# Chunks of 384 tokens in a fused attention and FFN kernel

## The chip, the cores and the metric

The kernel runs on one core of one Trainium2 chip. The metric is the device time of one execution in microseconds (us). A core has these engines, each with an in-order list of instructions of its own: TensorE (PE in the profile, with its weight loads as PEld), VectorE (DVE), ScalarE (ACT), GpSimd (POOL) and SyncE (SP), which here issues DMAs. Semaphores order them against each other.

## What is computed

```python
phi(x) = exp(h - max(h)) / sqrt(m)        # h = x*scale @ omega.T - |x*scale|^2/2, m = 128 features
kv  = phi(k)^T v                          # per batch and head, 128 x 64
z   = sum over s of phi(k)
att = phi(q) kv / (phi(q) . z + 1e-6)     # q, k, v: 8 batches, 8 heads, 576 tokens, 64 dims
x   = att as (4608 tokens) x (512 = heads x dims)
h   = x @ w_in                            # 512 -> 2048
out = (h - tanh(h)) @ w_out               # 2048 -> 512
```

All is fp32; a product of two fp32 matrices is made of three matmuls of rounded parts (hi x hi, hi x lo, lo x hi), so that most tiles have a hi and a lo (`xh` and `xl`, `gh` and `gl`, `qh` and `ql`).

## The kernel before

The FFN goes through the 4608 tokens in chunks of 256 (chunks 0 and 1 together, then 2 to 17). For a chunk, DFF = 2048 is cut into 16 slices `f` of 128 rows, taken two at a time (`s` from 0 to 7). For each `s`, `ffn_p` makes h of two slices in one PSUM bank (256 tokens each, 24 matmuls of 256 columns), `ffn_g` makes g = h - tanh(h) and its parts gh and gl on ACT and DVE (tanh, subtract, round, subtract), and `ffn_out` adds them to the two output tiles po0 and po1 (128 tokens x 512, 12 matmuls of 512 columns). In the loop, `ffn_out` of a step stands behind `ffn_h` of the next one: h(s+1), then out(s). Behind the last step of a chunk `ffn_store` copies the output tiles and stores them.

The attention of the next chunks runs beside it, in pieces that are generators. A `q_unit(ch, c)` makes the x of chunk `ch` for a pair of heads `c` (four pairs): it loads q, splits it in hi and lo (`split_rows`), projects it (`features`: pj on PE, a copy on ACT, a reduction on DVE, Exp on ACT), multiplies with z for the denominators `dn` on DVE, normalizes, transposes (pt on PE, then qh and ql), multiplies with kv (pn on PE, then copies and adds to `xs`), and `x_split` writes xh and xl. A `k_unit(b, c)` makes kv and z of a batch and a pair in a like way (ka, km and kb are its projections, khl and vhl its parts, pk its sums). Each `beat()`, two in a step, moves every open generator by one `yield`; the table `start` says at which beat a unit begins. x has two buffers, by the parity of the chunk.

The order on each engine is not the order of the code: up to the 14th slice of chunk 0 it is written out by hand (`ORDER`), and behind that a scheduler orders the instructions ahead of time, by its own estimate of when each is ready; on the chip every engine takes its list strictly in that order. PSUM has eight banks: h0 and h1 for h, po0 and po1 for the outputs, and for attention pj0 and pj1 (projections), pt (shared by pt and pn) and pk.

Of the kernel before, what the change touches and what calls it, by code (L numbers as in the profile page):

```python
# [81 lines left out]
def favor_attention_ffn(ctx: ExitStack, tc: tile.TileContext, qT, kT, va, vt, omT, w, out):  # L82
# [84 lines left out]
    def features(lhs, name):  # L167

        n = len(lhs)
        ph = att("phi", [P, 4, M], F32, f"phi_{name}")  # L170
        nb = sb.tile([P, 4], F32, tag="nb", name=f"nb_{name}", bufs=12)

        for g in range(0, n, 2):
            m = min(2, n - g)
            pj = ps.tile([P, 2, 2 * M], F32, tag=bank("pj"), name=f"pj_{name}_{g}")
            for i in range(m):
                nc.tensor.matmul(pj[:, i], lhs[g + i], om2, start=True, stop=True)  # L177
            nc.scalar.copy(ph[:, g : g + m], pj[:, :m, M:])  # L178
            for i in range(m):
                j = g + i  # L180
                nc.vector.tensor_tensor_reduce(  # L181
                    ph[:, j], pj[:, i, :M], ph[:, j], scale=-SCALE, scalar=3.0e38,
                    op0=ALU.add, op1=ALU.min, accum_out=nb[:, j : j + 1])
        for j in range(n):
            nc.scalar.activation(ph[:, j], ph[:, j], AF.Exp, bias=nb[:, j : j + 1], scale=-1.0)  # L185
        return ph
# [107 lines left out]

    def q_unit(ch, c):

        n = f"{ch}_{c}"
# [8 lines left out]
        ix = lambda h, t: 2 * h + t
        dn = sb.tile([P, 4], F32, tag="dn", name=f"dn_{n}", bufs=8)
        for h in range(2):
            for t in range(2):
                i = ix(h, t)  # L310
                for b, s, e in pieces:
                    s, e = max(s, t * P), min(e, (t + 1) * P)
                    if s < e:
# [1 line left out]
                        nc.vector.tensor_tensor_reduce(  # L315
                            bank("junk")[r], ph[r, i], kvs[b, c][1][r, h], scale=1.0, scalar=EPS,
                            op0=ALU.mult, op1=ALU.add, accum_out=dn[r, i : i + 1])
        nc.vector.reciprocal(dn, dn)
        nc.vector.tensor_mul(ph, ph, dn.rearrange("p (i o) -> p i o", o=1).to_broadcast([P, 4, M]))
# [4 lines left out]
        for i in range(4):
            nc.tensor.transpose(pt[:, i * P : (i + 1) * P], ph[:, ix(i // 2, i % 2)], ident)  # L325
# [4 lines left out]
        nc.vector.tensor_sub(ql, pt2, qh.bitcast(F32))  # L330
        yield
        pn = ps.tile([P, 2, TC], F32, tag=bank("pt"), name=f"pn_{n}")
        for h in range(2):
            for b, s, e in pieces:
                w = kvs[b, c][0][:, h * P : (h + 1) * P]
                nc.tensor.matmul(pn[:, h, s:e], w, qh[:, h, s:e], start=True, stop=False)  # L336
                nc.tensor.matmul(pn[:, h, s:e], w, ql[:, h, s:e], start=False, stop=True)  # L337
# [8 lines left out]
        xdone[ch] = xdone.get(ch, 0) + 1

    def x_split(ch, c, x, engine):
        nc.scalar.copy(xh[:, ch % 2, c], x)
        engine.tensor_sub(xl[:, ch % 2, c], x, xh[:, ch % 2, c].bitcast(F32))  # L350
# [10 lines left out]
    xh, xl = [sb.tile([P, 2, NC, TC], F32R, name=f"x{k}") for k in "hl"]  # L361

    def ffn_p(ch, s, tag):

        p = ps.tile([P, 2, TC], F32, tag=tag, name=f"h_{ch}_{s}")
        for j in range(1 if ch == 0 else 2):
            f = s if ch == 0 else 2 * s + j
            o = p if ch == 0 else p[:, j]
            r = slice(0, 2) if ch == 0 else ch % 2
            prods = [(wt[f][:, i, c * P : (c + 1) * P], x[:, r, c]) for c in range(NC)  # L370
                     for i, x in ((0, xh), (0, xl), (1, xh))]
            for i, (w_, x) in enumerate(prods):
                nc.tensor.matmul(o, w_, x, start=i == 0, stop=i == len(prods) - 1)  # L373
        return p

    def ffn_g(ch, s, p):

# [6 lines left out]
        nc.scalar.copy(gh, g)  # L384
# [10 lines left out]
    def ffn_out(ch, s, gh, gl):  # L395
        po = pos[ch]
        for t in range(len(po)):
            for j in ((t // 2,) if ch == 0 else range(2)):
                f = s if ch == 0 else 2 * s + j
                h = gh[:, j, t % 2 * P : (t % 2 + 1) * P]  # L400
                l = gl[:, j, t % 2 * P : (t % 2 + 1) * P]
# [1 line left out]
                nc.tensor.matmul(po[t], h, wt[f][:, 0, DM:], start=first, stop=False)  # L403
# [5 lines left out]
    def ffn_store(ch):  # L409
        for t, p in enumerate(pos[ch]):  # L410
            if ch == NCH - 1 and t == 1:
                o = sb.tile([P, DM], F32, tag="g", name=f"o_{ch}_{t}")
                nc.vector.tensor_copy(o, p)
            else:
                o = sb.tile([P, DM], F32, tag="o", name=f"o_{ch}_{t}")
                nc.scalar.copy(o, p)
            r = ch * TC + t * P
            nc.sync.dma_start(out[r : r + P, :], o)
# [126 lines left out]
    def native_q(ch, c):  # L545
# [47 lines left out]
        def x_hi():  # L593
# [3 lines left out]
            if c < 2:  # L597
                x2[c] = sb.tile([P, TC], F32, tag="xs", name=f"x2_{c}", bufs=2)
            elif 2 not in x2:
                o = sb.tile([P, DM], F32, tag="o", name="x2")  # L600
                x2[2], x2[3] = o[:, 0:TC], o[:, TC:]
            nc.scalar.copy(x2[c], u["pn"])
# [227 lines left out]
```

## Time and profile before

| what | value |
|---|---|
| median of 3 runs | 1062.15 us (1059.04 to 1064.06) |
| the profiled execution | 1060.27 us |
| its span, first to last instruction | 1058.5 us |
| mean granted TensorE clock | 0.995 |
| first h of chunk 2 / chunk 3 / chunk 4 | 174 / 229 / 290 us |
| last matmul | 1054 us |

The profile is of one execution. Its rows give, for a group of instructions, line, engine, operation, tiles out and in, shape and count, then the busy time, the mean of one in ns, and the idle time of the engine ahead of them with what ended it. In a timeline a row begins with start and duration in us. Matmuls are pipelined: a row's duration is longer than the distance from its start to the next one, and the distance is what the engine needs for it.

### The profile page before, as it was taken

The page shows a single profiled execution, that of the slowest core. Times are in us where ns is not written, and L with a number is a line of the kernel's source. Part 1 is how long each engine was busy: PE and PEld are TensorE (multiplying, and loading weights), DVE is VectorE, ACT ScalarE, POOL GpSimd, SP SyncE. Part 2 cuts the span into 40 slices and gives each one's busy share as a digit, 9 for nine tenths or more (in the row PEclk, how much of TensorE's full clock was granted, in tenths as well). Part 3 has the DMA queues.
Part 4 walks back from the last instruction along what each step waited for, and adds up shares of the span by engine and source line. Part 5 has one row for each costly group of instructions (what it writes and reads, how often), then busy time and mean ns, then how long its engine had stood idle before and what let it go on. Part 6 is the DMA issues. An engine that isn't in the chain of part 4 may idle for free.

```text
span 1058.5 us, 20071 instructions
## 1 busy us (share of the span) xinstructions
PE 1038.0 (98%) x6908; PEld 938.4 (89%) x6908; DVE 804.0 (76%) x2761; ACT 679.8 (64%) x1730; POOL 276.4 (26%) x445
## 2 busy tenths in 40 slices
PE   9999998999999999999999999999999999999998
PEld 7777677988999999999999998999999999999997
DVE  6888765766688886789899878998888887666522
ACT  7996665665576755576667766676777675555422
POOL 1127650001133410234333334343333331000000
PEclk9999999998999999999999999999999999999999
DMA  8998562100011110011111111111101010000000
GB/s 232 278 247 253 128 157 61 57 31 10 17 53 30 46 31 33 11 48 33 54 33 53 33 43 39 33 54 33 46 30 45 30 37 11 30 16 21 1 21 20
DMA packets 43462, 64.67 MB, mean 61 GB/s; under 512 B 18656, under 2 KB 28000, under 8 KB 41312
## 3 DMA queue, kind: packets, MB, share of 16 engines
q1 hardware_dynamic: 38672, 38.19, 12.1%
q10 hardware_dynamic: 2384, 16.81, 4.5%
q0 software_dynamic: 2304, 8.39, 4.3%
q8 instruction: 55, 0.90, 0.3%
q14 instruction: 47, 0.39, 0.1%
HBM read 45.55 MB, written 9.44 MB: 52 GB/s over the span
## 4 chain that ended last, share of the span: by engine, by line
PE 82%; DVE 7%; ACT 4%; issue 3%; DMA 2%; POOL 1%; DVEq 0%; ACTq 0%; POOLq 0%; SPq 0%
PE h L373 34%; PE po L403 11%; PE po L404 11%; PE po L405 11%; PE pj_q L177 3%; PE pt L325 2%; PE pk L236 2%; DMA w<-a 2%; PE pn L337 2%; PE pn L336 2%; DVE a L650 1%; ACT k_phi L491 1%; DVE a L658 1%; PE pj_ka L177 1%; PE pj_kb L177 1%
## 5 line engine op out<-in xcount | busy, mean ns | idle before, releaser
L373 PE MATMUL h<-xh,w 128*128 128x256 f32 (+1 forms) x2176 | 451.9, 292 | 3.7 <-DVE g L381 2.5
L373 PEld LDWEIGHTS h<-xh,w 128*128 128x128 f32 x2176 | 357.4, 192 | 14.2 <-DVE g L381 2.7
L373 PE MATMUL h<-xl,w 128*128 128x256 f32 (+1 forms) x1088 | 317.7, 292 | 0.6 <-DVE xl L350 0.6
L403 PE MATMUL po<-w,gh 128*128 128x512 f32 x544 | 213.9, 393 | 1.6 <-ACT gh L384 1.6
L373 PEld LDWEIGHTS h<-xl,w 128*128 128x128 f32 x1088 | 208.8, 192 | 7.1 <-DVE xl L350 0.9
L404 PE MATMUL po<-w,gh 128*128 128x512 f32 x544 | 213.6, 393 | 0.0
L405 PE MATMUL po<-w,gl 128*128 128x512 f32 x544 | 211.8, 391 | 1.4 <-DVE gl L387 1.4
L384 ACT CAST gh<-g 128x512 fp32r<-128x512 f32 x144 | 89.4, 621 | 100.0 <-DVE g L381 98.6
L381 DVE TENSOR_TENSOR g<-h,g 128x512 f32<-128x512 f32 x144 | 98.9, 687 | 67.5 <-ACT g L379 66.3
L379 ACT ACTIVATE g<-h 128x512 f32<-128x512 f32 x144 | 85.5, 594 | 99.6 <-PE h L373 93.3
L387 DVE TENSOR_TENSOR gl<-g,gh 128x512 fp32r<-128x512 f32 x144 | 109.0, 757 | 42.5 <-ACT gh L384 40.7
L405 PEld LDWEIGHTS po<-w,gl 128*128 128x128 f32 x544 | 102.3, 188 | 24.5 <-DVE gl L387 3.7
L403 PEld LDWEIGHTS po<-w,gh 128*128 128x128 f32 x544 | 102.5, 188 | 18.4 <-ACT gh L384 2.0
L404 PEld LDWEIGHTS po<-w,gh 128*128 128x128 f32 x544 | 102.5, 188 | 15.5
L185 ACT ACTIVATE phi_q<-phi_q,nb_q 128x128 f32<-128x128 f32 x240 | 78.8, 392 | 3.7 <-DVE nb_q L181 3.5
L330 DVE TENSOR_TENSOR ql<-pt,qh 128x512 fp32r<-128x512 f32 x60 | 41.2, 686 | 38.1 <-ACT qh L329 37.9
L315 DVE CUSTOM_DVE_ANT_0 junk<-phi_q,zb 128x128 f32<-128x128 f32 (+1 forms) x200 | 59.9, 300 | 11.3 <-ACT phi_q L185 0.3
L241 POOL TENSOR_TENSOR zt<-phi_ka 128x256 f32<-128x256 f32 x20 | 16.9, 846 | 184.6 <-ACT phi_ka L185 184.6
L638 POOL TENSOR_SCALAR a<-a 128x1024 f32<-128x1024 f32 x14 | 53.1, 3799 | 32.1 <-ACT a L627 32.0
L181 DVE CUSTOM_DVE_ANT_0 phi_q<-pj_q,phi_q 128x128 f32<-128x128 f32 x240 | 55.8, 283 | 5.5 <-ACT phi_q L178 5.4
L329 ACT CAST qh<-pt 128x512 fp32r<-128x512 f32 x60 | 35.0, 583 | 38.7 <-PE pt L325 38.5
L228 POOL CAST vhl<-v 128x128 fp32r<-128x128 f32 (+1 forms) x120 | 37.3, 313 | 77.6 <-PE pk L236 73.0
(158 smaller groups left out, 1846.7 us busy)
## 6 DMA issues: line engine op xcount, KB each, us to landing
raw<-w ACTq DMA_DIRECT2D x16, 1024.0 KB, 6.3
out<-o SPq DMA_DIRECT2D x36, 256.0 KB, 2.0
w<-a POOLq DMA_DIRECT2D x16, 512.0 KB, 5.7
qf<-qT SPq DMA_DIRECT2D x60, 128.0 KB, 2.1
kf<-kT SPq DMA_DIRECT2D x20, 288.0 KB, 2.8
v<-vt SPq DMA_DIRECT2D x20, 288.0 KB, 2.8
v<-va SPq DMA_DIRECT2D x12, 320.0 KB, 4.6
k_f<-kT SPq DMA_DIRECT2D x12, 288.0 KB, 3.9
```

Of the source, the lines that this page charges most:

```text
L181: nc.vector.tensor_tensor_reduce(ph[:, j], pj[:, i, :M], ph[:, j], scale=-SCALE, scalar=3.0e38, op0=ALU.add, op1=ALU.min, accum_out=nb[:, ...
L185: nc.scalar.activation(ph[:, j], ph[:, j], AF.Exp, bias=nb[:, j : j + 1], scale=-1.0)
L315: nc.vector.tensor_tensor_reduce(bank("junk")[r], ph[r, i], kvs[b, c][1][r, h], scale=1.0, scalar=EPS, op0=ALU.mult, op1=ALU.add, accum_ou ...
L373: nc.tensor.matmul(o, w_, x, start=i == 0, stop=i == len(prods) - 1)
L379: nc.scalar.activation(g, p, AF.Tanh)
L381: nc.vector.tensor_sub(g, p, g)
L384: nc.scalar.copy(gh, g)
L387: nc.vector.tensor_sub(gl, g, gh.bitcast(F32))
L403: nc.tensor.matmul(po[t], h, wt[f][:, 0, DM:], start=first, stop=False)
L404: nc.tensor.matmul(po[t], h, wt[f][:, 1, DM:], start=False, stop=False)
L405: nc.tensor.matmul(po[t], l, wt[f][:, 0, DM:], start=False, stop=last)
L638: engine.tensor_scalar(u["af"], u["af"], -TOP, TOP, op0=ALU.max, op1=ALU.min)
```

## The change

Chunk 2 keeps its 256 tokens; behind it ten chunks (3 to 12) have 384. For them

- h of one slice fills a bank: 12 matmuls of 384 columns, 16 steps a chunk, where there were 24 of 256 for two slices and 8 steps;
- a chunk has three output tiles, po0, po1 and pj1, with 9 out matmuls a step. Attention keeps three banks: pj0, pt and pk;
- a `q_unit` has 384 tokens: three rounds of projection through pj0, each in a beat of its own, and pt, pn, copy and add for each head of the pair in turn through the bank pt;
- one tile each takes the place of several small ones (`zf`, `zr`: ident, junk, g, gh, gl, o, xs and others are slices of them), and most attention tiles have one buffer: qf one and not two, xs one and not two, phi two for q and one each for k's;
- the starting beats are new: chunk `ch` begins at beat 32 ch - 48, and its four q units at 32 ch - 87 + 8 c.

```diff
-NS = NF // 2
 TC = 256
-NCH = NT // TC
+TW = 384
+START = [0, TC, 2 * TC, *range(3 * TC, NT, TW)]
+NCH = len(START)
+WB = TW // P
...
 def features(lhs, name):
     n = len(lhs)
-    ph = att("phi", [P, 4, M], F32, f"phi_{name}")
+    kind, w = ("phq", 2 * WB) if name[0] == "q" else ("phm", 1) if n == 1 else ("phk", 4)
+    ph = att(kind, [P, w, M], F32, f"phi_{name}")
     for g in range(0, n, 2):
+        if g:
+            yield
...
 def q_unit(ch, c):
-    x = att("qx", [P, 2, TC], F32R, f"qx_{n}")
+    if ch > 3:
+        yield
+    x = att("qx", [P, 2, TW], F32R, f"qx_{n}")
...
-    pt = ps.tile([P, 2 * TC], F32, tag=bank("pt"), name=f"pt_{n}")
-    for i in range(4):
-        nc.tensor.transpose(pt[:, i * P : (i + 1) * P], ph[:, ix(i // 2, i % 2)], ident)
+    xs = zf[:, 8 : 8 + WB]
     for h in range(2):
+        pt = ps.tile([P, TW], F32, tag=bank("pt"), name=f"pt_{n}_{h}")
+        for t in range(WB):
+            nc.tensor.transpose(pt[:, t * P : (t + 1) * P], ph[:, 2 * t + h], ident)
+        nc.scalar.copy(qh, pt)
+        nc.vector.tensor_sub(ql, pt, qh.bitcast(F32))
+        yield
+        pn = ps.tile([P, TW], F32, tag=bank("pt"), name=f"pn_{n}_{h}")
         for b, s, e in pieces:
-            nc.tensor.matmul(pn[:, h, s:e], w, qh[:, h, s:e], start=True, stop=False)
-            nc.tensor.matmul(pn[:, h, s:e], w, ql[:, h, s:e], start=False, stop=True)
+            nc.tensor.matmul(pn[:, s:e], w, qh[:, s:e], start=True, stop=False)
+            nc.tensor.matmul(pn[:, s:e], w, ql[:, s:e], start=False, stop=True)
+        nc.scalar.copy(xs[r], blocks(pn)[o])
+        nc.vector.tensor_add(xs[r], blocks(pn)[r], xs[r])
+        yield
...
-    phi=(ak, 3), qh=(ak, 1), ql=(ak, 1), tmp=(ak, 1), kf=(ak, 1), kx=(ak, 1), qf=(ak, 2),
+    phq=(ak, 2), phk=(ak, 1), phm=(ak, 1), qh=(ak, 1), ql=(ak, 1), kf=(ak, 1), kx=(ak, 1), qf=(ak, 1),
...
-        k = [28,30,33,35][c] if ch == 3 else [42,45,48,52][c] if ch == 4 else 16 * (ch - 1) - 6 + 4 * c
+        k = [28, 31, 34, 37][c] if ch == 3 else 32 * ch - 87 + 8 * c
...
-        k = 28 + 5 * c if b == 2 else 16 * (need[b] - 1) - 25 + 8 * c
+        start.setdefault(48 * b - 89 + 12 * c, []).append(("k", b, c))
...
 for ch in range(2, NCH):
-    out_tiles(ch)
-    for s in range(NS):
+    if ch == 3:
+        mode.update(pj=["pj0"])
+    out_tiles(ch, ("po0", "po1") if ch == 2 else ("po0", "po1", "pj1"))
+    for s in range(8 if ch == 2 else NF):
```

How it moves instructions shows best where a chunk begins. PE before, from the last out matmuls of chunk 6 into chunk 7 (`po1_6` is an output tile of chunk 6, `h_7_1` the second step of chunk 7; all of `h_7_0` stands ahead of these rows):

```order
L404 MATMUL po1_6_4795<-w15_1760,gh_6_7_5423 128x512
L336 MATMUL pn_8_0_5532<-qh_8_0_5473,kvw_3_0_3281 128x256
L337 MATMUL pn_8_0_5532<-ql_8_0_5474,kvw_3_0_3281 128x256
L336 MATMUL pn_8_0_5532<-qh_8_0_5473,kvw_3_0_3281 128x256
L337 MATMUL pn_8_0_5532<-ql_8_0_5474,kvw_3_0_3281 128x256
L405 MATMUL po1_6_4795<-w15_1760,gl_6_7_5425 128x512
L373 MATMUL h_7_1_5613<-xh_100,w2_497 128x256
L373 MATMUL h_7_1_5613<-xl_101,w2_497 128x256
```

PE after, at the entry into its chunk 7: the last out matmul of chunk 6 (`pj1_6`) stands some rows ahead of these, and so do the products of `h_7_0` and `h_7_1` with pairs 0 to 2; `pt_7_3` and `pn_7_3` make the x of pair 3, `pj_kb5_1` and `pk_5_1` belong to k of batch 5, and the two rows of L403 are the first products of h with pair 3:

```order
L335 MATMUL pt_7_3_0_6399<-zf_68,phi_q7_3_6270 128x128 x3
L184 MATMUL pj_kb5_1_0_6471<-om_96,kx_5_1_6280 128x256 x2
L243 MATMUL pk_5_1_6303<-khl_5_1_2_6373,vhl_5_1_2_6374 128x256 x2
L243 MATMUL pk_5_1_6303<-khl_5_1_4_6432,vhl_5_1_4_6433 128x256 x2
L344 MATMUL pn_7_3_0_6427<-qh_7_3_0_6403,kvw_4_3_5832 128x384
L345 MATMUL pn_7_3_0_6427<-ql_7_3_0_6404,kvw_4_3_5832 128x384
...
L335 MATMUL pt_7_3_1_6461<-zf_68,phi_q7_3_6270 128x128 x3
L184 MATMUL pj_q8_0_0_6547<-om_96,qx_8_0_6504 128x256 x2
L344 MATMUL pn_7_3_1_6488<-qh_7_3_1_6465,kvw_4_3_5832 128x384
...
L403 MATMUL h_7_0_6647<-xb_1783,w0_971 128x384
L403 MATMUL h_7_1_6712<-xb_1783,w1_1066 128x384
L184 MATMUL pj_q8_0_4_6612<-om_96,qx_8_0_6504 128x256 x2
```

What was attention for chunk 8 between the matmuls of chunks 6 and 7 is now attention for chunk 7 itself, between chunk 6 and the end of h of chunk 7's first two slices.

DVE after at the same place, from the last gl of chunk 6 (L418; `zr` and `zf` hold g, `phi_q7_3` is the last pair of chunk 7):

```order
L418 TENSOR_TENSOR zr_67<-zf_68,zr_67 128x384
L324 ISA zf_68,dn_7_3_6340<-phi_q7_3_6270,zb_4_3_5830 128x128
...
L348 TENSOR_TENSOR zf_68<-pn_7_2_0_6185,zf_68 64x384
...
L328 TENSOR_TENSOR phi_q7_3_6270<-phi_q7_3_6270,dn_7_3_6340 128x768
...
L348 TENSOR_TENSOR zf_68<-pn_7_3_1_6488,zf_68 64x384
...
L359 TENSOR_TENSOR xb_1783<-zf_68,xb_1783 128x384
...
L414 TENSOR_TENSOR zf_68<-h_7_0_6647,zf_68 128x384
```

Between the gl of one chunk and the first g of the next (L414) lies the attention of the last pairs. DVE before, the same stretch whole:

```order
L387 TENSOR_TENSOR gl_6_7_5425<-g_6_7_5420,gh_6_7_5423 128x512
L330 TENSOR_TENSOR ql_8_0_5474<-pt_8_0_5468,qh_8_0_5473 128x512
L265 CAST zhl_4_0_5462<-zs_4_0_5178 128x256
L229 TENSOR_TENSOR vhl_4_1_0_5646<-v_4_1_5484,vhl_4_1_0_5646 128x2x64
L381 TENSOR_TENSOR g_7_0_5513<-h_7_0_5488,g_7_0_5513 128x512
```

Here the three operations between gl and g are for chunk 8 and for k.

More of the change, by code (lines that the diff above doesn't have):

```diff
@@ L131, in load @@
         nc.sync.dma_start(dst, src)
-    ident = const.tile([P, P], F32, name="ident")
-    junk = const.tile([P, M], F32, name="junk")
+    zp = ctx.enter_context(tc.tile_pool(name="zp", bufs=1))
+    zr = zp.tile([P, 16, P], F32R, name="zr")
+    zf = zp.tile([P, 16, P], F32, name="zf")
+    ident, junk = zf[:, 12], zf[:, 13]
     nc.vector.memset(junk, 0.0)
@@ L143, in favor_attention_ffn @@
     a0 = open_pool("a0")
-    omf = a0.tile([P, M], F32, name="omf")
+    omf = zf[:, 14]
     nc.sync.dma_start(omf[0:D], omT)
@@ L242, in zsum @@
             nc.gpsimd.tensor_add(zs[:, h], zt[:, 0], zt[:, 1])
-        pa = features(tiles[0:4], f"ka{n}")
+        pa = yield from features(tiles[0:4], f"ka{n}")
         yield
@@ L248, in k_single @@
         yield
-        pm = features(tiles[4:5], f"km{n}")
+        pm = yield from features(tiles[4:5], f"km{n}")
         kv(0, ku, True, False)
@@ L253, in k_single @@
         yield
-        pb = features(tiles[5:9], f"kb{n}")
+        pb = yield from features(tiles[5:9], f"kb{n}")
         kv(0, km[:1], False, True)
@@ L286, in pieces_of @@
     def pieces_of(ch):
-        t0 = t = ch * TC
+        t0 = t = START[ch]
+        n = TC if ch < 3 else TW
         pieces = []
-        while t < t0 + TC:
-            e = min((t // S + 1) * S, t0 + TC)
+        while t < t0 + n:
+            e = min((t // S + 1) * S, t0 + n)
             pieces.append((t // S, t - t0, e - t0))
@@ L348, in x_split @@
     def x_split(ch, c, x, engine):
-        nc.scalar.copy(xh[:, ch % 2, c], x)
-        engine.tensor_sub(xl[:, ch % 2, c], x, xh[:, ch % 2, c].bitcast(F32))
+        hi, lo = (blocks(y) for y in x_of(ch, c))
+        nc.scalar.copy(hi, x)
+        engine.tensor_sub(lo, x, hi.bitcast(F32))
     wt = {}
@@ L376, in ffn_g @@
     def ffn_g(ch, s, p):
-        g = sb.tile([P, 2, TC], F32, tag="g", name=f"g_{ch}_{s}")
+        n = 4 if ch < 3 else WB
+        p = blocks(p)[:, 0:n]
+        g = zf[:, 0:n]
+        gh, gl = (zr[:, k + s % 2 * 4 : k + s % 2 * 4 + n] for k in (0, 8))
         nc.scalar.activation(g, p, AF.Tanh)
@@ L397, in ffn_out @@
         for t in range(len(po)):
[L398 to L401, printed above, removed]
+            for j, f in enumerate(slices_of(ch, s)):
                 first, last = f == 0, f == NF - 1
-                nc.tensor.matmul(po[t], h, wt[f][:, 0, DM:], start=first, stop=False)
-                nc.tensor.matmul(po[t], h, wt[f][:, 1, DM:], start=False, stop=False)
-                nc.tensor.matmul(po[t], l, wt[f][:, 0, DM:], start=False, stop=last)
+                nc.tensor.matmul(po[t], gh[:, 2 * j + t], wt[f][:, 0, DM:], start=first, stop=False)
+                nc.tensor.matmul(po[t], gh[:, 2 * j + t], wt[f][:, 1, DM:], start=False, stop=False)
+                nc.tensor.matmul(po[t], gl[:, 2 * j + t], wt[f][:, 0, DM:], start=False, stop=last)
     pos = {}
@@ L410, in ffn_store @@
         for t, p in enumerate(pos[ch]):
+            o = xb[1] if ch > 2 and t == 1 else zf[:, 4:8]
+            if ch == NCH - 1 and t == 2:
+                o = zf[:, 8:12]
             if ch == NCH - 1 and t == 1:
-                o = sb.tile([P, DM], F32, tag="g", name=f"o_{ch}_{t}")
-                nc.vector.tensor_copy(o, p)
-            else:
[L415 to L418, printed above, removed]
+                nc.vector.tensor_copy(o, blocks(p))
+            else:
+                nc.scalar.copy(o, blocks(p))
+            r = START[ch] + t * P
+            nc.sync.dma_start(blocks(out[r : r + P, :]), o)
     def out_tiles(ch, tags=("po0", "po1")):
         pos[ch] = [ps.tile([P, DM], F32, tag=t, name=f"{t}_{ch}") for t in tags]
-    need = {b: (b * S) // TC for b in range(B)}
     xdone = {}
@@ L553, in den @@
         def den():
-            dn = u["dn"] = sb.tile([P, 4], F32, tag="dn", name=f"{n}_dn", bufs=8)
+            dn = u["dn"] = sb.tile([P, 2 * WB], F32, tag="dn", name=f"{n}_dn", bufs=8)[:, 0:4]
             for t in range(2):
@@ L596, in x_hi @@
                 return
[L597 to L602, printed above, removed]
+            x2[c] = zf[:, (8, 10, 4, 6)[c] : (10, 12, 6, 8)[c]]
+            nc.scalar.copy(x2[c], blocks(u["pn"]))
         def x_lo():
@@ L737, in favor_attention_ffn @@
     ak = open_pool("ak")
+    xb[0] = ak.tile([P, 6 * TW], F32R, name="xb")
+    xb[1] = ak.tile([P, DM // P, P], F32, name="o1")
     mode.update(
```

94 lines of the change are left out of this document (48 added, 46 removed).

## The prediction

> **What bounds the kernel now.** I read the page first, then the busy time by stage, then rows of the timeline. The page (engines' busy time, then the span in 40 slices):
>
> ```profile
> PE 1038.0 (98%) x6908; PEld 938.4 (89%) x6908; DVE 804.0 (76%) x2761; ACT 679.8 (64%) x1730; POOL 276.4 (26%) x445
> PE   9999998999999999999999999999999999999998
> PEclk9999999998999999999999999999999999999999
> ```
>
> The stages (busy time and count on PE, PEld, DVE, ACT, POOL, then the granted clock):
>
> ```profile
> 228.00:234.50 6.50, 6.50 (x44) 5.93 (x43) 4.80 (x22) 3.70 (x11) 0.00 (x0) 1.00 0.16 58
> 234.50:241.10 6.60, 3.08 (x17) 1.97 (x15) 5.15 (x24) 6.06 (x17) 0.00 (x0) 0.82 0.20 63
> 241.10:245.50 4.40, 4.40 (x20) 4.40 (x21) 3.87 (x21) 1.99 (x5) 0.00 (x0) 0.50 0.10 30
> 250.00:1050.00 800.00, 799.30 (x5418) 739.28 (x5417) 617.25 (x2238) 499.29 (x1296) 207.53 (x398) 1.00 0.10 32
> ```
>
> From 250 to 1050 us PE has no hole, so its instructions are the time: an instruction less is time gained, and any wait put in front of PE is lost in full. DVE is 77% busy there. The one hole behind 228 us is the entry into chunk 3, and what made it is the pattern to look for.
>
> **Wider h matmuls.** Rows of PE without attention, chunk 17 (start, duration):
>
> ```profile
> 1009.71 0.40 PE L403 MATMUL po<-w,gh 128*128 128x512 f32 x1
> ...
> 1012.45 0.28 PE L373 MATMUL h<-xh,w 128*128 128x256 f32 x1
> 1012.57 0.28 PE L373 MATMUL h<-xl,w 128*128 128x256 f32 x1
> ...
> 1014.85 0.40 PE L373 MATMUL h<-xh,w 128*128 128x256 f32 x2
> ```
>
> From start to start, 20 matmuls of 256 columns take 2.40 us, 0.120 each; 12 of 512 columns take 2.74 us, 0.228 each. 384 columns lie midway: 0.174 (ends 0.171, three quarters of the one, and 0.180, one and a half of the other). Chunks 3 on hold 3840 tokens: 15 x 8 x 24 = 2880 matmuls of 256 become 10 x 16 x 12 = 1920 of 384: 345.6 - 334.1 = 11.5 us less (0 to 17). The out matmuls stay 1440 of 512.
>
> A rule against this: the Trainium skill, "TensorE: Matmul & The Clock Gate", section "Back-to-back issue gap", gives a warm matmul its columns at 2.4 GHz and 2.5 ns more, so 109 and 162 ns here; two for three would save 2 ns, 2 us in all and not 11.5. The rows have 120 ns where it has 109, so I go by them.
>
> **pn.** The list of PE's instructions has 320 pn matmuls before, 160 of 256 columns and 160 narrower, and 208 after, 112 of 384 and 96 of 192 (three of ten chunks, not five of fifteen, lie across two batches). A narrow one takes 0.11:
>
> ```profile
> 245.83 0.28 PE L336 MATMUL pn<-qh,k_kvw 128*128 128x128 f32 x1
> 245.94 0.28 PE L337 MATMUL pn<-ql,k_kvw 128*128 128x128 f32 x1
> ```
>
> 160 x 0.12 + 160 x 0.11 = 36.8; 112 x 0.174 + 96 x 0.115 (between the two) = 30.5: 6.3 less. pj, pt and pk keep their numbers and widths.
>
> **The entries into chunks.** This is the term that decides. In the order before, from chunk 4 on, the matmuls of h follow the last slice of the chunk before directly; the x that they need was ready long ago. In the order after, for every chunk from 3 to 12, the attention of the chunk's own last pairs stands on PE behind the last out matmuls of the chunk before and ahead of h's last products. PE works its list in order, so it has to sit through that chain. Before has this once, into chunk 3:
>
> ```profile
> 236.42 0.94 PE L177 MATMUL pj_q<-om,qx 128*128 128x256 f32 x4 [1.26 <-DVE qx L164]
> 238.27 0.68 PE L325 MATMUL pt<-ident,phi_q 128*128 128x128 f32 x4 [0.92 <-ACT phi_q L185]
> 239.74 0.79 PE L373 MATMUL h<-xh,w 128*128 128x256 f32 x2 [0.79 <-ACT xh L349]
> 241.09 0.58 PE L373 MATMUL h<-xl,w 128*128 128x256 f32 x1 [0.56 <-DVE xl L350]
> ```
>
> 17 matmuls at 0.12 are 2.0 us of the 6.6, so 4.6 are lost, and 2.0 more at half clock (20 matmuls in 4.4 us): 6.6 in all. That hole goes and its successor is priced with the others.
>
> What DVE must do between the last gl of a chunk and the last x of the next bounds the wait, because DVE too works in order. Its spacing, from rows of the same stretch:
>
> ```profile
> 227.75 0.69 DVE L387 TENSOR_TENSOR gl<-g,gh 128x512 fp32r<-128x512 f32 x1 [0.36 <-ACT gh L384]
> 229.29 0.29 DVE L181 CUSTOM_DVE_ANT_0 phi_q<-pj_q,phi_q 128x128 f32<-128x128 f32 x1
> 229.50 0.29 DVE L181 CUSTOM_DVE_ANT_0 phi_q<-pj_q,phi_q 128x128 f32<-128x128 f32 x1
> 230.04 0.42 DVE L164 TENSOR_TENSOR qx<-qf,qx 64x256 fp32r<-64x256 f32 x1
> 230.49 0.42 DVE L165 TENSOR_TENSOR qx<-qf,qx 64x256 fp32r<-64x256 f32 x1
> 234.90 0.29 DVE L181 CUSTOM_DVE_ANT_0 phi_q<-pj_q,phi_q 128x128 f32<-128x128 f32 x1 [1.01 <-ACT phi_q L178]
> 238.16 0.29 DVE L315 CUSTOM_DVE_ANT_0 junk<-phi_q,k_zb 128x128 f32<-128x128 f32 x1
> 238.60 0.29 DVE L315 CUSTOM_DVE_ANT_0 junk<-phi_q,k_zb 128x128 f32<-128x128 f32 x1
> 240.61 0.42 DVE L350 TENSOR_TENSOR xl<-xs,xh 128x256 fp32r<-128x256 f32 x1
> 240.95 0.17 DVE L318 RECIPROCAL dn<-dn 128x4 f32<-128x4 f32 x1
> 242.18 0.69 DVE L319 TENSOR_TENSOR phi_q<-phi_q,dn 128x512 f32<-128x512 f32 x1
> 242.78 0.28 DVE L181 CUSTOM_DVE_ANT_0 phi_q<-pj_q,phi_q 128x128 f32<-128x128 f32 x1
> ```
>
> So a reduction of L181 takes 0.21, one of the denominators 0.21 to 0.44 (I take 0.26), a 64x256 operation 0.45, 128x256 0.34, 128x512 0.60; hence 128x384 0.47, 64x384 0.57, 128x768 0.87. K's side, from another stretch:
>
> ```profile
> 303.17 0.28 DVE L219 CAST khl<-phi_ka 128x256 fp32r<-128x256 f32 x1
> 303.37 0.68 DVE L381 TENSOR_TENSOR g<-h,g 128x512 f32<-128x512 f32 x1
> ...
> 316.60 0.75 DVE L164 TENSOR_TENSOR kx<-kf,kx 64x576 fp32r<-64x576 f32 x1
> 317.38 1.19 DVE L165 TENSOR_TENSOR kx<-kf,kx 64x576 fp32r<-64x576 f32 x1
> ```
>
> A khl (or vhl) 0.2, a kx 0.78. Into chunk 7 the order has on DVE, from gl of slice 15 to the last x: 17 reductions 3.6, 8 denominators and reciprocal 2.2, the normalization 0.9, 5 operations of 128x384 2.4, 6 of 64x384 3.4, 2 kx 1.6, 12 khl and vhl 2.5, 5 small ones 1.2: 17.8 us. On PE stand there, behind the last out matmul: 17 pj, 14 pk and ones, 13 transposes, 6 pn, 12 h: 3.7 + 1.4 + 3.1 = 8.2 us. Counted in the same way, DVE has 16.5, 7.2, 22.2, 19.0, 17.8, 21.8, 18.7, 17.8 and 18.9 us for the entries into chunks 3 to 11 (159.9), and PE 7.6, 3.8, 10.0, 6.6, 8.2, 9.3, 6.6, 8.2 and 8.1 (68.4). Of DVE's time some 2 us lie beside the last slice's 9 out matmuls (9 x 0.228). Low end, with DVE never idle: 159.9 - 68.4 - 9 x 2 = 73.5 us of waiting. DVE is idle, though: before, the same list from 228.44 to 241.03 is 9.85 us of work in 12.6, a ratio of 1.28. With it: 118. One wait in that stretch, 1.01 us at 234.90, goes back to PE being busy with h and out, which it no longer is: 1.18 without it. And there DVE had little but that one chain, while now k's pieces stand among the operations of the last pair and fill half of the rest: I take 1.1, 175.9 - 86.4 = 89.5. The last entry, into chunk 12, has only one pn ahead: 2.5 us for its copy, add and two halves of x. Sum 92 (ends 76 and 121).
>
> **The clock at the entries.** The profile has two stretches of 5 us in which PE is busy for about half of the time, and a third with 3.21:
>
> ```profile
> 65.00:70.00 5.00, 3.21 (x28) 2.61 (x28) 4.96 (x10) 4.83 (x14) 1.34 (x2) 1.00 0.90 219
> 170.00:175.00 5.00, 2.51 (x12) 2.08 (x11) 4.50 (x14) 4.07 (x10) 0.00 (x0) 0.89 0.20 59
> 235.00:240.00 5.00, 2.04 (x11) 1.27 (x10) 4.00 (x20) 4.84 (x14) 0.00 (x0) 0.87 0.25 79
> ```
>
> The clock stays at 1.00 in the third and falls in the two, and the row of 241.1 to 245.5 shows what follows: 20 matmuls in 4.4 us at 0.50, 2.0 us lost. At the entry into chunk 7 PE has some 8 us of work in 18, less than half: I expect the same 2.0 us at each of nine entries, 18 (0 if it stays; up to 22 if half clock lasts longer).
>
> **What else moves.** Slices are shorter, with three operations in a row from h to gh (groups of the page: busy us, mean ns, idle before them and what ended it):
>
> ```profile
> L384 ACT CAST gh<-g 128x512 fp32r<-128x512 f32 x144 | 89.4, 621 | 100.0 <-DVE g L381 98.6
> L381 DVE TENSOR_TENSOR g<-h,g 128x512 f32<-128x512 f32 x144 | 98.9, 687 | 67.5 <-ACT g L379 66.3
> L379 ACT ACTIVATE g<-h 128x512 f32<-128x512 f32 x144 | 85.5, 594 | 99.6 <-PE h L373 93.3
> ```
>
> 1.9 us before, about 1.5 at 384. Their cover is the out matmuls of the slice before and the next h: 12 x 0.228 + 24 x 0.12 = 5.6 us before, 9 x 0.228 + 12 x 0.174 = 4.1 after. It still holds on free engines; behind other work on ACT and DVE some slices will be late. I take 3 us (0 to 10, a hundred slices of 0.1). The loads of q go from 60 of 128 KB to 40 of 192; each is issued beats ahead of its use and costs nothing while that lead is there. The third output tile shares a buffer with the first, so its copy waits for a store on ACT, ahead of qh and the exps:
>
> ```profile
> ACT o L416 <- DMA out<-o: 10.1, 10, 2.1
> ```
>
> (waiter, releaser: us in total, times, longest.) That wait is there before too, up to 2.1 us once a chunk; at an entry it lies inside the chain priced above. The stages up to 165 us keep their order, and the tail (three stores, the last copy on ACT) its length: 0.
>
> **Sum.** 1058.5 - 11.5 - 6.3 - 6.6 + 92 + 18 + 3 = 1147.1 us of span. The profiled execution is 1.8 longer than its span, and the median of the runs is 1.9 above it, within their spread of 5.0; I forecast 1149 us, slower by 8%.
>
> **Rivals.**
> Not slower: every entry costs no more than the one into chunk 12, because DVE and ACT have all but the last pn behind them when PE arrives. 10 x 2.5 = 25, and the clock holds: 1058.5 - 24.4 + 25 + 3 = 1062, and 1064 with the 1.8: no change. It decides below 3 us an entry. Against it stands the order: the last round of the last pair's projection (`pj_q7_3_4`) is itself behind the last out matmuls on PE, and its reductions, exps, denominators, transposes and pn can't begin earlier. With no wait at all it would be 1039. Chance 0.08 for both.
> The clock holds: the pj and pk of k break the waits up, so that no stretch is as empty as the two above. Then 18 less, 1131. For it: the row of 65 to 70 us. Chance 0.22. The Trainium skill ("TensorE: Matmul & The Clock Gate", "Why this matters for your kernels") asks for idle gaps above some 3 us between bursts of matmuls before the clock falls; by that rule it would hold here. In this trace holes of at most 1.3 us, 4.6 together, were enough.
> The wide matmul saves nothing, because time goes by columns and a step at a time: 0.180 for 384, 11.5 us more, 1160. Chance 0.08. The Trainium skill's rule on the issue gap, above, would give 1158 (an estimate by that page).
> Forecast as it stands, with entries of 7 to 13 us and the clock falling: 0.62.
>
> **How the numbers follow.** Low: entries at 6 us, little more than half of the taken value, and the clock holding, gives 1131 - 38 = 1093. High: 121 at the entries, 22 of clock, 10 of late slices, 1149 + 29 + 4 + 7 = 1189; I take 1180, since the three seldom come together. About 0.5%, 5 us, is what a measurement here can tell from no change. Faster: the rival without waits, 0.04; no change 0.04; slower the rest.
>
> **What would show it.** In the profile after: h of 128x384 starting every 0.174 us; PE's slices with nine dips some 90 us apart; in each, PE waiting for DVE and ACT (phi_q, x, khl) with DVE near full; PE full between them, and PEclk at 0.5 for some 4 us behind each. I am wrong if PE is 98% busy again, if the dips are under 5 us, or if late gh fills the middle of the chunks with waits.

## The result: 1216 us, and where the time went

The changed kernel takes 1216.39 us (median of 4 runs, 1213.33 to 1219.20), the one before 1060.97 beside it: a ratio of 1.1455, interval 1.1423 to 1.1486. It is slower, as forecast, but by 155 us and not by 87; 1149 was forecast, with a range up to 1180.

The page after (engines' busy time, then PE and its clock in 40 slices):

```profile
PE 1110.1 (91%) x5836; PEld 973.9 (80%) x5836; DVE 806.2 (66%) x2721; ACT 701.6 (58%) x1730; POOL 274.6 (23%) x445
PE   9999989889999869979998996997899799699998
PEclk9989999979989959988996997899799699799899
```

PE has the dips that were forecast, some 100 us apart, and the clock falls in each. By stage, about the entry into chunk 7 (busy time and count on PE, PEld, DVE, ACT, POOL, then the granted clock):

```profile
560.00:620.00 60.00, 60.00 (x324) 54.86 (x323) 38.15 (x131) 31.87 (x78) 10.99 (x23) 1.00 0.08 22
630.87:654.63 23.76, 16.90 (x63) 13.48 (x62) 19.02 (x82) 17.49 (x46) 10.11 (x20) 0.61 0.21 67
654.63:660.00 5.37, 3.90 (x13) 3.54 (x13) 5.04 (x18) 3.44 (x11) 0.52 (x1) 0.50 0.11 37
660.00:720.00 60.00, 60.00 (x328) 54.77 (x328) 37.07 (x133) 31.19 (x77) 11.10 (x25) 1.00 0.06 17
```

Between the entries PE is full. The entry itself, from the last out matmul of chunk 6 (630.87) to the last product of h of chunk 7's first two slices (654.63), takes 23.8 us for 63 matmuls, which are 8.3 us at the spacing that matmuls of their widths have elsewhere.

For the whole kernel I charge each matmul behind 229 us with the median distance that matmuls of its width have to the next start in these two traces (0.120 us for 256 columns, 0.175 for 384, 0.229 for 512, 0.109 for 128) and call the rest lost. Before: 815.9 us of matmuls and 9.6 lost. After: 804.3 and 179.0. So the matmuls became 11.6 us shorter and 169.4 us more are lost. The two sums add up to the time behind 229 us by construction, so this doesn't test the split, and 0.001 us more a matmul moves some 4 us from one to the other: with mean distances (0.1194 us for h before, 0.1757 after) the matmuls became 7.7 us shorter. Of the 179.0, the ten entries hold 176.6: 151.0 inside them and 25.6 in the 60 matmuls behind each.

What an entry is made of shows in the rows of one resource, the bank of the projections. First two rounds in the middle of a chunk, PE's matmuls of L184 and the last reduction of each (L188 on DVE), which frees the bank:

```profile
567.59 0.48 PE L184 MATMUL pj_q<-om,qx 128*128 128x256 f32 x2
569.68 0.28 DVE L188 CUSTOM_DVE_ANT_0 phi_q<-pj_q,phi_q 128x128 f32<-128x128 f32 x1
572.84 0.40 PE L184 MATMUL pj_q<-om,qx 128*128 128x256 f32 x2
574.35 0.29 DVE L188 CUSTOM_DVE_ANT_0 phi_q<-pj_q,phi_q 128x128 f32<-128x128 f32 x1
577.76 0.40 PE L184 MATMUL pj_q<-om,qx 128*128 128x256 f32 x2
```

The bank is free at 569.96 and 574.64, but PE's list has the next projection only at 572.84 and 577.76, one FFN step (5 us) behind the last. Over 100 such rounds the median distance is 5.13 us, and the bank is in use for 1.55 of it. Now the same at the entry into chunk 7:

```profile
631.80 0.48 PE L184 MATMUL pj_ka<-om,kx 128*128 128x256 f32 x2
633.28 0.28 DVE L188 CUSTOM_DVE_ANT_0 phi_ka<-pj_ka,phi_ka 128x128 f32<-128x128 f32 x1
633.72 0.47 PE L184 MATMUL pj_q<-om,qx 128*128 128x256 f32 x2
635.81 0.29 DVE L188 CUSTOM_DVE_ANT_0 phi_q<-pj_q,phi_q 128x128 f32<-128x128 f32 x1
636.25 0.71 PE L184 MATMUL pj_ka<-om,kx 128*128 128x256 f32 x2
638.41 0.28 DVE L188 CUSTOM_DVE_ANT_0 phi_ka<-pj_ka,phi_ka 128x128 f32<-128x128 f32 x1
639.44 0.41 PE L184 MATMUL pj_km<-om,kx 128*128 128x256 f32 x1
641.72 0.78 PE L184 MATMUL pj_kb<-om,kx 128*128 128x256 f32 x2
644.35 0.63 PE L184 MATMUL pj_kb<-om,kx 128*128 128x256 f32 x2
646.38 0.78 PE L184 MATMUL pj_q<-om,qx 128*128 128x256 f32 x2
649.29 0.74 PE L184 MATMUL pj_q<-om,qx 128*128 128x256 f32 x2
652.39 0.63 PE L184 MATMUL pj_q<-om,qx 128*128 128x256 f32 x2
```

Nine rounds follow each other nearly as fast as the bank comes free, each over PE, a copy on ACT and reductions on DVE: over 68 such pairs the median distance is 2.30 us and the bank is free for 0.16 of it. The arithmetic behind this: a chunk of 384 needs 4 x 3 rounds for q and 2.67 x 5 for k, 25.3; it has 16 steps, and one bank gets one round a step. The list of PE's instructions has 15 or 16 rounds between two entries, and the others, 5 to 13 and 9.5 in the mean, at the entry. Before, two banks took 16.9 rounds in the 8 steps of a chunk.

Not all nine rounds are on the way to chunk 7. Its own last round is the second of them (the `pj_q` at 633.72, `pj_q7_3_4` in the list); the other eight are for batch 5 and chunk 8, and seven of them stand behind it. What follows it for chunk 7, on DVE (denominators, normalization, the parts and the sum of a head, the last x):

```profile
639.32 0.19 DVE L327 RECIPROCAL dn<-dn 128x6 f32<-128x6 f32 x1
642.61 0.56 DVE L339 TENSOR_TENSOR ql<-pt,qh 128x384 fp32r<-128x384 f32 x1 [0.42 <-ACT qh L338]
645.09 0.55 DVE L348 TENSOR_TENSOR zf<-pn,zf 64x384 f32<-64x384 f32 x1 [0.46 <-ACT zf L347]
652.31 0.55 DVE L359 TENSOR_TENSOR xb<-zf,xb 128x384 fp32r<-128x384 f32 x1
```

So from the start of that round to the last x it takes 19.1 us. For the entries into chunks 5 to 11 the chunk's own last round starts 2.8 to 11.2 us behind the last out matmul, and the last x comes 17.1 to 19.6 us after it; into chunk 4 it starts 9.8 us ahead, and that entry takes 10.6 us. What the one bank does to an entry is to make this round late, and then the rest of the chain lies behind the last out matmul too.

### The profile page after: what moved, and what is told of

The parts are those of the page before. It is cut to its first block, busy times and chain, and to the rows that moved or that the text cites. A ratio compares the mean times of both kernels' runs of the same rounds, so it can differ in the third digit from the quotient of the medians.

```text
span 1217.4 us, 17780 instructions
## 1 busy us (share of the span) xinstructions
PE 1110.1 (91%) x5836; PEld 973.9 (80%) x5836; DVE 806.2 (66%) x2721; ACT 701.6 (58%) x1730; POOL 274.6 (23%) x445
## 3 DMA queue, kind: packets, MB, share of 16 engines
q1 hardware_dynamic: 35792, 38.18, 10.6%
## 4 chain that ended last, share of the span: by engine, by line
PE 71%; DVE 12%; ACT 10%; issue 3%; POOL 2%; DMA 2%; DVEq 0%; ACTq 0%; POOLq 0%
PE h L403 30%; PE po L431 7%; PE po L432 7%; PE po L433 7%; PE pj L432 3%; PE pj L431 3%; PE pj L433 3%; PE pt L335 2%; PE pj_q L184 2%; PE pk L243 2%; ACT k_phi L519 1%; PE pn L344 1%; DVE zf L324 1%; PE pn L345 1%; DVE a L682 1%
## 5 line engine op out<-in xcount | busy, mean ns | idle before, releaser
L403 PE MATMUL h<-xa,w 128*128 128x384 f32 (+2 forms) x1584 | 335.4, 349 | 14.3 <-DVE zf L414 7.0
L403 PEld LDWEIGHTS h<-xa,w 128*128 128x128 f32 x1584 | 281.4, 197 | 34.5 <-ACT xa L358 8.3
L414 DVE TENSOR_TENSOR zf<-h,zf 128x384 f32<-128x384 f32 (+1 forms) x184 | 105.3, 572 | 138.9 <-ACT zf L412 137.2
L412 ACT ACTIVATE zf<-h 128x384 f32<-128x384 f32 (+1 forms) x184 | 92.7, 504 | 171.9 <-PE h L403 158.5
L403 PE MATMUL h<-xb,w 128*128 128x384 f32 x720 | 162.1, 356 | 5.0 <-ACT xb L358 4.9
L431 PE MATMUL po<-w,zr 128*128 128x512 f32 x384 | 151.8, 395 | 1.5 <-ACT zr L416 1.5
L432 PE MATMUL po<-w,zr 128*128 128x512 f32 x384 | 151.3, 394 | 0.0
L433 PE MATMUL po<-w,zr 128*128 128x512 f32 x384 | 143.0, 396 | 1.4 <-DVE zr L418 1.4
L403 PEld LDWEIGHTS h<-xb,w 128*128 128x128 f32 x720 | 135.3, 200 | 11.0 <-ACT xb L358 6.1
L416 ACT CAST zr<-zf 128x384 fp32r<-128x384 f32 (+1 forms) x184 | 97.3, 529 | 77.6 <-DVE zf L414 73.4
L418 DVE TENSOR_TENSOR zr<-zf,zr 128x384 fp32r<-128x384 f32 (+1 forms) x184 | 112.2, 610 | 44.5 <-ACT zr L416 41.3
L433 PEld LDWEIGHTS po<-w,zr 128*128 128x128 f32 x384 | 71.0, 188 | 15.7 <-DVE zr L418 3.3
L431 PEld LDWEIGHTS po<-w,zr 128*128 128x128 f32 x384 | 72.3, 188 | 10.3 <-ACT zr L416 1.9
L432 PEld LDWEIGHTS po<-w,zr 128*128 128x128 f32 x384 | 72.2, 188 | 8.6
L184 PE MATMUL pj_q<-om,qx 128*128 128x256 f32 x240 | 60.7, 338 | 15.8 <-DVE nb_q L188 9.2
L188 DVE CUSTOM_DVE_ANT_0 phi_q<-pj_q,phi_q 128x128 f32<-128x128 f32 x240 | 59.4, 285 | 21.2 <-ACT phi_q L185 20.1
```

Of the source, the lines that this page charges most:

```text
L188: nc.vector.tensor_tensor_reduce(ph[:, j], pj[:, i, :M], ph[:, j], scale=-SCALE, scalar=3.0e38, op0=ALU.add, op1=ALU.min, accum_out=nb[:, ...
L412: nc.scalar.activation(g, p, AF.Tanh)
L414: nc.vector.tensor_sub(g, p, g)
L418: nc.vector.tensor_sub(gl, g, gh.bitcast(F32))
L431: nc.tensor.matmul(po[t], gh[:, 2 * j + t], wt[f][:, 0, DM:], start=first, stop=False)
L432: nc.tensor.matmul(po[t], gh[:, 2 * j + t], wt[f][:, 1, DM:], start=False, stop=False)
```

## The experiments

The theory: one projection bank gets one round a step, and what does not fit runs at the entry, where a round comes every 2.5 us in the mean. Rivals: the units begin too late; the bank of the transposes or the chain of a unit is the limit; DVE's work sets the entry (my prediction); the clock does. This table puts the kernels side by side: rounds in PE's list between two entries (chunks 4 to 10), rounds at entries 4 to 11, the length of these eight entries, when the chunk's own last round starts against the last out matmul of the chunk before (entries 5 to 11; a minus is ahead of it), and what all ten entries lose by the charge above, the 60 matmuls behind each included. The changed kernel and e4 have four runs each, the others in the table one, and the changed kernel's four lie 6 us apart: a difference of that size says nothing.

| kernel | rounds between | rounds at entries | eight entries, us | own last round, us | lost, us | time, us |
|---|---|---|---|---|---|---|
| after | 15, 16 | 76 | 195.3 | +2.8 to +11.2 | 176.6 | 1216.39 |
| e1 two projection banks | 20 to 24 | 25 | 45.3 | -29.3 to -26.9 | 58.3 | 1104.81 |
| e2 two transpose banks | 15, 16 | 77 | 192.1 | +4.5 to +12.8 | 161.1 | 1205.70 |
| e3 units start earlier | 14 to 16 | 76 | 197.5 | +1.2 to +9.6 | 175.5 | 1218.93 |
| e4 h one bank, projections two | 17 to 25 | 9 | 24.7 | -53.8 to -47.9 | 22.5 | 1076.71 |
| e5 one projection a round | 15, 16 | 248 (halves) | 453.9 | +38.0 to +47.6 | 394.2 | 1437.01 |
| e6 h one bank alone | 15, 16 | 75 | 215.1 | +0.6 to +5.8 | 169.9 | 1215.11 |
| e7 entries kept warm | 16 | 69 | 183.7 | -3.4 to +5.8 | 66.5 | 1193.69 |
| e8 no k units | 9, 10 | 21 | 44.9 | -26.3 to -22.4 | 61.8 | 1045.41 |

**e1: the bank given back.** The third output tile's products go to the second tile, and projections rotate through two banks:

```diff
-                first, last = f == 0, f == NF - 1
+                first, last = f == 0 and (t < 2 or ch < 2), f == NF - 1 and t != (1 if ch > 2 else 9)
...
+        if ch > 2:
+            pos[ch].append(pos[ch][1])
...
-            mode.update(pj=["pj0"])
-        out_tiles(ch, ("po0", "po1") if ch == 2 else ("po0", "po1", "pj1"))
+            mode.update(pj=["pj0", "pj1"])
+        out_tiles(ch, ("po0", "po1"))
```

> The third output tile's products are added to the second tile (the same matmuls, its 128 tokens of a chunk are not computed rightly), so that the eighth bank is free and projections (pj) rotate through two banks as before. Theory, one projection bank: between two entries PE's list holds 15 or 16 rounds of two projections a chunk, one a step, and 9.4 more stand at the entry; with two banks only 1 to 5 stand there. Entries fall from about 20 us to under 5 each from chunk 4 on, time 1050 to 1090 us. Rival, units begin too late: nothing changes, 1216. Rival, the bank of the transposes: nothing changes, 1216.

1104.81 us. The entry into chunk 7 and the chunk behind it:

```profile
600.20:603.80 3.60, 3.34 (x19) 2.55 (x18) 2.77 (x11) 3.14 (x10) 1.92 (x5) 1.00 0.37 139
603.80:684.50 80.70, 79.95 (x452) 73.43 (x452) 65.77 (x252) 52.77 (x141) 25.56 (x48) 1.00 0.11 30
```

Its 23.8 us became 3.6, with the same matmuls of FFN. The time is 15 us above the range that I gave: the entry into chunk 3 loses 17 us here too, and the entries into 5, 8 and 11 take 8 to 9 us and not under 5. They lose 4 to 5 us inside, in waits of up to 2.7 us for DVE, and 1 to 2 behind.

**e2: the same bank given to the transposes.** As e1, but

```diff
-            mode.update(pj=["pj0"])
+            mode.update(pj=["pj0"], pt=["pt", "pj1"])
```

> As the kernel with two projection banks, but the free bank goes to transposes and pn (pt), projections keep one. Theory, one projection bank: the list still has 9 to 13 rounds at the entries, 1216 within 20 us. Rival, the chain of pt, qh, ql and pn through one bank: entries fall to under 5 us, 1050 to 1090.

1205.70 us, and 77 rounds at the entries: it is not any eighth bank that helps, but one for projections. The 11 us less than the changed kernel come from a single run.

**e3: earlier starts.**

```diff
-            k = [28, 31, 34, 37][c] if ch == 3 else 32 * ch - 87 + 8 * c
+            k = [28, 31, 34, 37][c] if ch == 3 else (32 * ch - 87 if ch == 4 else 32 * ch - 91) + 8 * c
-            start.setdefault(48 * b - 89 + 12 * c, []).append(("k", b, c))
+            start.setdefault(48 * b - 93 + 12 * c, []).append(("k", b, c))
```

> All q units from chunk 5 on and all k units begin 4 beats (two steps, some 10 us) earlier; more is not possible, since x of a chunk would overwrite x of the chunk two before. Theory, one projection bank: a head start is used up once and the rounds that do not fit stay (the list has 8 to 11 at each entry), 1216 within 25 us. Rival, units begin too late: each of eight entries is up to 10 us shorter, about 1135 us.

1218.93 us: nothing gained. The entry into chunk 5 fell from 31.9 to 19.7 us and the one into chunk 4 rose from 10.6 to 21.5; from chunk 7 on the last rounds are about as late as before. A head start is used up once; the rate stays.

**e4: the bank taken from h.** Here all outputs are computed:

```diff
-            mode.update(pj=["pj0"])
+            mode.update(h=["h0"], pj=["pj0", "h1"])
```

> From chunk 3 on h has one bank and projections two (pj0 and h1); everything is computed. Theory, one projection bank: entries from chunk 4 on lose at most 2 us each, the one into chunk 3 some 15; the one bank of h is free after tanh and the subtraction, 1.1 us beside 2.05 us of out matmuls, and costs 0 to 10 us. 1217 - 179 + 15 + 5 = 1058 us, between 1045 and 1070. Rival, the second bank of h is what keeps PE full: 0.5 us and more lost in each of 160 steps, 1130 or above. Rival, units begin too late: 1216.

1076.71 us (4 runs), 1.0156 of before (1.0139 to 1.0173), 7 us above the range that I gave. The entry into chunk 3, and all behind 270 us, then the latter of the kernel before:

```profile
233.70:262.20 28.50, 18.79 (x71) 14.55 (x70) 23.09 (x94) 18.18 (x49) 4.00 (x8) 0.70 0.12 39
270.00:1070.00 800.00, 791.90 (x4347) 721.66 (x4346) 600.84 (x2152) 492.42 (x1274) 217.33 (x386) 1.00 0.11 31
```

```profile
270.00:1050.00 780.00, 779.30 (x5292) 721.26 (x5291) 608.28 (x2216) 491.74 (x1278) 204.44 (x394) 1.00 0.11 33
```

From chunk 4 on no entry loses more than 1.2 us. What is left is the entry into chunk 3 (18.6 us, 15 forecast) and some 12 us ahead of h's matmuls (0 to 10 forecast), in waits for its one bank such as

```profile
408.88 2.36 PE L403 MATMUL h<-xa,w 128*128 128x384 f32 x12 [0.57 <-DVE zf L414]
```

**e5: twice the rounds.** A round holds one projection:

```diff
-        for g in range(0, n, 2):
-            if g:
+        for g in range(0, n, ROUND[0]):
+            if g and g % 2 == 0:
                 yield
-            m = min(2, n - g)
+            m = min(ROUND[0], n - g)
...
+            ROUND[0] = 1
```

> From chunk 3 on a round holds one projection and not two: the same matmuls and reductions, twice the rounds for q, nine for five for k. Theory, one round a step through the one bank: the list still has 15 or 16 rounds between two entries, and 19 to 34 at an entry (248 in entries 4 to 11, 76 before). At 2.2 to 2.6 us each the eight entries take 545 to 645 us where they took 195: 1560 to 1670 us. Rival, the entry costs what DVE and ACT have to do there (the predicted sum): their work grows by some 200 copies of 0.2 us, 1216 to 1260.

1437.01 us. A chunk and the entry into chunk 7:

```profile
624.70:694.30 69.60, 69.28 (x359) 62.62 (x358) 36.59 (x108) 32.79 (x79) 9.95 (x20) 0.99 0.05 12
694.34:747.43 53.09, 31.77 (x102) 23.65 (x100) 33.66 (x137) 32.39 (x89) 16.39 (x34) 0.60 0.15 43
```

Between the entries there are still 15 or 16 rounds, and 30 at this entry, which grew from 23.8 to 53.1 us. DVE is busy for 63% of it, and for 80% before. The rival that sums DVE's work (1216 to 1260) is out as I put it, but it left out that DVE's work moves to the entries with the rounds: the eight entries hold 292 us of it here and 160 in the changed kernel. At the changed kernel's 1.22 us of entry for each of these they would take 356 us; they take 454. So DVE's work alone doesn't set them, though it is a good part. My size was wrong too: a round of one costs 1.75 us there (the slope over these eight entries), not 2.2 to 2.6.

**e6: the control for e4.**

```diff
-            mode.update(pj=["pj0"])
+            mode.update(h=["h0"], pj=["pj0"])
```

> h has one bank from chunk 3 on, as in the version with two projection banks, but the freed bank stays empty and projections have one. Theory: 75 rounds at entries 4 to 11 in the list (76 before), so 1200 to 1245 us. Rival, that version gained by the one bank of h and not by the second one of projections: below 1100.

1215.11 us: the 138 us between e6 and e4 are those of the second projection bank.

**e7: the clock.** On e6, ten transposes into the empty bank `h1` behind each round that stands at an entry in its list:

```diff
+            if f"{name}_{g}" in AT_ENTRY:
+                for i in range(10):
+                    nc.tensor.transpose(spare[0][:, i % 4 * P : (i % 4 + 1) * P], ph[:, g], ident)
```

> As the kernel with one bank of h alone, and ten transposes into the empty bank behind each round that stands at an entry (about 75 rounds, 1 us each at full clock, results unused), so that PE is busy there for more than half of the time. If the clock at half speed makes the entries longer (27 us behind them, and PE's part of each round doubled, 68 us of work at most), the clock stays near 1.0 and the time falls by 20 to 70 us against the kernel with one bank of h alone. If the entries are only the chain over ACT and DVE, the time stays or rises by up to 75 us.

The entry into chunk 7 in e6, then in e7:

```profile
630.94:658.41 27.47, 19.11 (x63) 14.53 (x62) 22.58 (x88) 18.66 (x48) 9.80 (x20) 0.59 0.22 65
```

```profile
630.73:651.91 21.18, 19.02 (x136) 16.53 (x135) 19.15 (x78) 15.50 (x41) 8.08 (x15) 1.00 0.27 85
```

The clock stays at 1.00, and with 83 us of added matmuls the kernel is 21 us faster (1193.69), at the low end of the 20 to 70 forecast. The list also has six rounds fewer at the entries, worth some 15 at 2.5 each, so the clock's own part of the 21 us isn't separated from theirs, nor from what the transposes cost. But with the clock at full speed the eight entries still take 183.7 us where they took 215.1: it is not what makes the entries long.

**e8: fewer rounds.**

```diff
     def k_unit(b, c):
+        if b > 2:
+            kvs[b, c] = kvs[2, c]
+            yield
+            return
```

> k units of batches 3 to 7 left out (kv and z of batch 2 are used for them): 12 rounds a chunk through the one bank instead of 25.3. Theory, one round a step: 12 fit into 16 steps, no projection of the chunk's own is left at its entry, which costs some 3 us for the last pn, as the entry into chunk 12 does now. 55 us of PE work go too: 1217 - 179 + 15 + 9 x 3 - 55 = 1025 us (1010 to 1050). Rival, the chain of a q unit itself (single buffers, bank pt) is too long for its chunk: entries stay at 10 us or more, 1090 and above.

1045.41 us, within the range. With 12 rounds a chunk the one bank is enough from chunk 4 on: 9 or 10 stand between the entries, the 2 or 3 at an entry are the next chunk's, and the chunk's own last round starts 22 us and more ahead. The chain of a q unit is not the limit. This run also takes k's work from DVE and ACT, so it can't tell the bank from that work; e1 against e2 and e4 against e6 can. The entry into chunk 7:

```profile
565.82:571.08 5.26, 3.80 (x21) 2.79 (x19) 4.00 (x18) 4.49 (x13) 0.00 (x0) 1.00 0.44 162
```

**e9 and e10: what the theory is good for.** The rule should hold for any bank. Chunk 2 has 8 steps, and the x of chunk 3 needs 16 turns of the bank pt; the bank pk is idle then.

```diff
-            if g:
+            if g and name[:3] != "q3_":
                 yield
...
-    mode.update(pj=["pj0", "pj1"], pt=["pt"])
+    mode.update(pj=["pj0", "pj1"], pt=["pt", "pk"])
...
-            mode.update(pj=["pj0"])
+            mode.update(h=["h0"], pj=["pj0", "h1"], pt=["pt"])
```

> The version with one bank of h and two for projections, and in chunk 2 the bank pk, idle there, as a second one for transposes and pn; the rounds of the units of chunk 3 follow each other without a beat between. Theory, one turn a step through each bank: chunk 2 has 8 steps and the x of chunk 3 needs 16 turns of pt and pn; with one bank half of them stand at the entry into chunk 3 (18.6 us lost), with two one pn. 13 us less than 1077: 1064 (1058 to 1068). Rival, the units of chunk 3 begin too late for any bank: 1077.

1063.96 us (10 runs), 1.0033 of before (1.0016 to 1.0049). The entry into chunk 3:

```profile
237.10:250.60 13.50, 10.36 (x42) 8.19 (x41) 12.56 (x63) 11.10 (x32) 5.33 (x10) 0.79 0.16 53
```

13.5 us where e4 has 28.5, and the time is the one forecast. The second bank and the beat taken out came together, so no run shows what each is worth. Then e10 adds

```diff
+        if ch == 4:
+            mode.update(hi=nc.gpsimd)
```

> As e9, and from chunk 4 on the hi parts of qx and kx are made on GpSimd, not on ScalarE. Theory: the 20 us still lost between the entries (waits of 0.3 to 0.8 us of h for the subtraction that frees its one bank, tanh being late behind these copies, 1.4 us for a kx) shrink by a half: 1050 to 1058. If GpSimd's copies make kx and qx late or take SBUF time from VectorE: 1064 to 1075.

1062.10 us (10 runs), 0.9999 of before (0.9979 to 1.0020): no measurable difference from the kernel before, and in neither of the ranges that I gave. So chunks of 384 can be had at no loss, with their banks divided in another way, but no version here beats the kernel before: in e9 the shorter matmuls are given back at the entry into chunk 3 (some 8 us) and ahead of h's matmuls (13 us by the charge above), where the waits that the trace names are for the one bank of h.

## Why the prediction was right and where it failed

- **Wider h and pn: right in kind, too large in size.** -11.5 and -6.3 were forecast, 17.8 for both; the traces give 8 to 12 for all matmuls, h 6 to 10 of it. Twelve matmuls of 384 from 1194.97 take 2.11 us, 0.176 each (0.174 forecast), and over 1920 of them 0.002 is 4 us:

```profile
1194.97 2.27 PE L403 MATMUL h<-xa,w 128*128 128x384 f32 x12
1197.08 0.39 PE L431 MATMUL po<-w,zr 128*128 128x512 f32 x1
```

- **Where the time is lost: right.** At the ten entries, in the order's own places, with PE full between them. The rivals "not slower" and "wide matmuls save nothing" are out.
- **The size of the entries: wrong, and this is the term that failed.** The step is "k's pieces stand among the operations of the last pair and fill half of the rest: I take 1.1". For chunks 3 to 11 it gave 1.1 x 159.9 - 18 = 158 us from the last out matmul to the last x; measured are 204.3 (217.2 to the last product of h). From the last gl to the last x it takes 244.0 us, 1.53 times those 159.9. DVE is busy for 180.8 of the 244.0, so its work was priced 21 us low (for chunk 7 19.8 and not 17.8), and idle for 63.2 where the 1.1 allowed 16. Of that idle time 48 us end with ACT, 28 of them with its copies out of pt and pn, as in the rows of DVE above. K's pieces did not fill these waits. The last out matmul of a chunk also came later, 4.4 us behind the last gl and not 2. Inside the nine entries 148 us are lost, and 89.5 were forecast.

  The bound that I took was DVE's. The chain that ends the entry into chunk 7 runs on DVE for 10.9 of its 23.8 us, on ACT for 4.7, on PE for 4.1 and on GpSimd for 2.7: no one engine's work sets it. And I had the order, with the pair's last round behind the last out matmul, but not why it stood there: I had looked for a bank that makes a wait, and not for how often a bank is used in a chunk and how often in a step. e1 and e4 show that this decides whether the entries are long at all. Whether the seven rounds behind chunk 7's own last one lengthen its 19.1 us, by taking time on ACT and DVE, or only fill its waits, no run here separates.
- **The clock: it fell, as forecast, but earlier.** 18 us (at most 22) were forecast behind the entries; 25.6 are lost there, and the clock is at one half inside them too, which the forecast left out. The rival that the clock holds is out. PE's longest wait in the entry into chunk 7 is 1.47 us:

```profile
635.66 0.50 PE L243 MATMUL pk<-khl,vhl 128*128 128x256 f32 x2 [1.47 <-POOL khl L227]
```

  The rule of the Trainium skill ("TensorE: Matmul & The Clock Gate", "Why this matters for your kernels") with its gaps of some 3 us would have let it hold. This trace decides against it: in this entry the clock fell with no longer wait, and in e7, with PE busy for 90% of the same stretch, it stayed at 1.00. The two stages of the entry about the fall:

```profile
630.87:636.30 5.43, 2.94 (x18) 2.08 (x16) 3.30 (x16) 5.19 (x14) 0.80 (x2) 1.00 0.39 145
636.30:660.20 23.90, 18.06 (x59) 15.14 (x60) 20.91 (x84) 15.78 (x44) 10.03 (x20) 0.50 0.15 42
```

- **Late slices: about right.** 179.0 - 176.6 = 2.4 us are lost elsewhere, as near as this charge can tell; 3 were forecast.
- **The range.** Its high end summed 121 for the entries, 22 for the clock and 10 for late slices. Measured are 151.0 inside the entries and 25.6 behind. Both ends came from DVE's 159.9 us and from the ratio at the one entry before, 1.28 there; with the 180.8 that DVE was busy the ratio is 1.35.

Not settled: why the scheduler gives a bank one round a step although it is free for 3.6 of 5.1 us. The runs show only that it does, whether a round holds two projections or one.

## What to carry to other kernels

Before a buffer or bank is taken away, count its uses in one period of the loop, and count in the order how many of them get a place in a step: what does not fit comes back at the loop's next dependence. Look there for the last use that the dependence needs, how late it starts, and how long its whole chain over all engines takes from there; the work of the busiest engine is too small a bound. Here that was 3 to 11 us and 17 to 20. A head start does not help against a rate, and a bank is worth most to the work that has more rounds than places: the same eighth bank was worth 112 us to projections and 11, from one run, to transposes.

## What was not expected of the hardware

The clock fell to 0.50 at the entry into chunk 7 with no wait of PE above 1.5 us, after 5.4 us in which PE was busy for 2.9, and stayed at 1.00 in the same stretch of e7, where PE was busy for 19.0 of 21.2 us. Filling the waits with 83 us of useless transposes, with six rounds fewer at the entries, made e6 21 us faster.
